# A decode-attention kernel: TensorE's closing part moved to the head of its program, one GpSimd library, x loaded by SyncE

## The chip, the core and the metric

The kernel runs on one core of one Trainium2 chip. The metric is the time of one execution on the device in microseconds (us), as the median of several runs. A core has five engines that run programs of their own and meet through semaphores: TensorE (PE in the profile, with PEld for its weight loads), VectorE (DVE), ScalarE (ACT), GpSimd (POOL) and SyncE (SP). Data moves between the main memory and the core's own memory through 16 DMA engines, which all queues share.

## What is computed

Two blocks of attention for one new token each, with the same shapes: a batch of 2, 32 heads, 8192 keys of 192 elements, a model width of 640, all bf16. `_B_ref` is the same as `_A_ref` here, since both have 32 heads of keys. The outputs of the two blocks are set side by side.

```python
q = (x @ wq).reshape(B, Sq, H, Dh).transpose(0, 2, 1, 3)          # x: 2 x 1 x 640, wq: 640 x 6144
scores = jnp.einsum("bhqd,bhkd->bhqk", q, k_cache) * (Dh ** -0.5) # k_cache: 2 x 32 x 8192 x 192
p = _softmax(scores, axis=-1)
o = jnp.einsum("bhqk,bhkd->bhqd", p, v_cache)
out = o.transpose(0, 2, 1, 3).reshape(B, Sq, H * Dh) @ wo         # wo: 6144 x 640
...
return jnp.concatenate([a, b], axis=-1)
```

## The kernel before

**Tiling.** The heads are taken in pairs: 2 blocks x 2 rows of the batch x 16 pairs are 64 pairs. For one pair, k (and likewise v) is one load of 6 MB: 128 partitions of 128 keys of 192 elements, the upper 64 partitions for one head, the lower 64 for the other. Three tiles `ring` take turns: the two large pieces of wq (4 of 5 rows per partition), then k and v of the pairs in order, at the end the pieces of wo. The fifth rows of wq go to the two tiles `prod`, which later hold products.

**Order of the work.** Each engine's instructions are collected in a `_Stream` in program order, with the keys that each waits for and the key that it signals; `reg` maps a key to a semaphore and a value. `emit` writes a stream out. For TensorE, VectorE and ScalarE it writes the part ahead of the loop (setup, projections and pair 0), a hardware loop `eng.Fori` of 21 passes over three pairs each (`LOOP`), and then the closing part, `self.run(eng, self.ops[at[n]:], {})`. SyncE and GpSimd have their streams written out without a loop.

**Start.** SyncE issues the loads in order (`load_on`, L196): A's large piece of wq, A's fifth rows, B's large piece, B's fifth rows, the first k; the next v waits until A's projection has read its slot, and so on. The load of the fifth rows waits for key `("x",)`. ScalarE issues the two small loads of x (L240) on its own queue. GpSimd fills the constants: the identity `ident` (a memset and an affine select, L402 and L403), `sel`, `place`, zeros for `pb` and so on, and signals `init` at its end (L418). TensorE opens the accumulation tile `oall` (L424, waits for `init`), transposes x (`fn_x`, L429; ScalarE copies it to `xT`) and projects each block in 12 groups of 5 matmuls (L260), which ScalarE copies to `qrow`.

**One pair.** VectorE multiplies k with the broadcast q in four quarters (L291); TensorE sums the 192 products in 12 matmuls of 16 columns a quarter (L296); VectorE reduces the rest (L302) and takes the maximum (L307, L308); GpSimd spreads the maximum over the partitions by `partition_all_reduce` (L311); ScalarE computes the exponentials (L323); TensorE multiplies with v in 64 matmuls (L335). TensorE also runs 12 matmuls on constants in each pair (`add_fill`, L343). The result of a pair is normalized on VectorE (L356 to L360) and put in its columns of `oall` by four small matmuls (`place`, L372) in the next pair.

**Closing part.** The last pair is placed (L372), `oall` is closed (L473) and copied to `oallS` (L378), and the 48 rows of wo of each block are contracted in 96 matmuls of 320 columns (L387), B's in eight pieces, so that the last ones can follow their loads; a few matmuls on constants stand between them. ScalarE copies each block's result out of `outps` (L395), and SyncE and ScalarE each issue one half of the output (L398).

Of the kernel before, what the change touches and what calls it, by code (L numbers as in the profile page):

```python
# [9 lines left out]
F32 = mybir.dt.float32  # L10


class _Stream:
# [40 lines left out]
            if has_sig:  # L54
                ins.then_inc(self.sem, 1)

    def emit(self, eng, loop=None):
        waited = {}
        if self.first:
            eng.sem_inc(self.sem, self.first)  # L60
        if loop is None:
            self.run(eng, self.ops, waited)
            return
        i0, step, n = loop
        at = [self.marks[i0 + step * t] for t in range(n + 1)]
        size = at[1] - at[0]
        passes = [self.ops[at[t]:at[t + 1]] for t in range(n)]
        needs = [[self.needs(w) for _, w, _ in ops] for ops in passes]
        delta = [{sid: needs[2][k][sid][1] - val for sid, (_, val) in need.items()} for k, need in enumerate(needs[1])]
        by, early = {}, {}  # L70
        for k, d in enumerate(delta):
            for sid, v in d.items():
                assert by.setdefault(sid, v) == v or not v or not by[sid]
                by[sid] = max(by[sid], v)
            for t, need in enumerate(needs):
                assert len(passes[t]) == size and passes[t][k][2] == passes[0][k][2]
                assert set(need[k]) == set(d) or t == 0 and set(need[k]) < set(d)
                for sid, (sem, val) in need[k].items():
                    plain = needs[1][k][sid][1] + (t - 1) * d[sid]
                    assert val == plain or t == 0 and val > plain  # L80
                    if val > plain:
                        early[sid] = (sem, max(val, early.get(sid, (sem, 0))[1]))
        self.run(eng, self.ops[:at[0]], waited)
        for sid, (sem, val) in early.items():
            if val > waited.get(sid, 0):
                eng.wait_ge(sem, val)
                waited[sid] = val
        for k, need in enumerate(needs[1]):
            for sid, (sem, val) in need.items():
                if not delta[k][sid] and val > waited.get(sid, 0):  # L90
                    eng.wait_ge(sem, val)
                    waited[sid] = val
        with eng.Fori(0, n) as t:
            base = {sid: eng.snap(t * d) for sid, d in by.items() if d}
            waited = {}
            for k, (fn, _, has_sig) in enumerate(passes[0]):
                for sid, (sem, val) in needs[1][k].items():
                    at0 = val - delta[k][sid]
                    if delta[k][sid] and at0 > waited.get(sid, 0):
                        eng.wait_ge(sem, base[sid] + at0)  # L100
                        waited[sid] = at0
                    assert not delta[k][sid] or at0 > 0
                ins = fn(eng, t)
                if has_sig:
                    ins.then_inc(self.sem, 1)
        self.run(eng, self.ops[at[n]:], {})


def build_kernel(nc, blocks, out):
    NBLK = len(blocks)  # L110
# [10 lines left out]
    LOOP = (1, STEP, 21)  # L121
# [5 lines left out]
    N = Hn * Dh  # L127
    RW = T * Dh
# [13 lines left out]
    with ExitStack() as es:  # L142
        sb = lambda name, shape, dt: es.enter_context(nc.sbuf_tensor(name, shape, dt))
# [8 lines left out]
        prod = [sb(f"prod{i}", [128, TQ * Dh], BF16) for i in range(2)]  # L152
# [9 lines left out]
        xr = sb("xr", [4, D], BF16)  # L162
# [5 lines left out]
        oallS = [sb(f"oallS{k}", [128, WR, 2], BF16) for k in range(NBLK)]  # L168
        out_sb = [sb(f"out_sb{k}", [34, NH2], BF16) for k in range(NBLK)]
        actd = sb("actd", [128, 2], F32)  # L170

        scps = [ps(f"scps{i}", [128, TQ, DG], F32) for i in range(2)]
        ops = [ps(f"ops{i}", [128, 512], F32) for i in range(NB)]
# [4 lines left out]
        reg = {}  # L178
        S_sp = _Stream("sp", sem("s_sp"), reg)
        S_pe = _Stream("pe", sem("s_pe"), reg, FIRST)  # L180
        S_act = _Stream("act", sem("s_act"), reg, FIRST)
        S_dve = _Stream("dve", sem("s_dve"), reg, FIRST)
        S_pool = _Stream("pool", sem("s_pool"), reg, FIRST)
        rsem = [sem(f"rsem{i}") for i in range(3)]
        psem = [sem(f"psem{i}") for i in range(2)]
        xsem = sem("xsem")
# [3 lines left out]
        def load(key, slot, out_ap, in_ap, waits):  # L190
            rcount[slot] += 16
            reg[key] = (rsem[slot], rcount[slot])
            load_on(out_ap, in_ap, rsem[slot], waits)

        def load_on(out_ap, in_ap, s, waits=()):
            S_sp.add(lambda eng, t: eng.dma_start(out_ap, in_ap).then_inc(s, 16), waits=waits)  # L196
# [8 lines left out]
        def next_slot(n=[0]):  # L205
            n[0] += 1
            return (n[0] - 1) % 3

        for blk in range(NBLK):
            w = blocks[blk]["wq"].rearrange("(j c) n -> j (c n)", c=DC)  # L210
            s = next_slot()
            load(("wq", blk), s, ring[s][:], w[:, 0:RW], [])
            reg[("wq5", blk)] = (psem[blk], 16)
            load_on(prod[blk][:, 0:N], w[:, RW:RW + N], psem[blk], [("x",)])
            free[s] = [("pr", blk, NQC - 1)]

        order = []
# [10 lines left out]
        for blk, pieces in ((0, WA), (1, WB)):  # L228
            w = blocks[blk]["wo"].rearrange("(p r) n -> p (r n)", r=WR)
# [4 lines left out]
                for r in range(r0, r1):  # L234
                    wo_at[blk, r] = ring[s][:, (at + r - r0) * D:(at + r - r0 + 1) * D]

        reg[("x",)] = (xsem, 32)
        for blk in range(NBLK):
            reg[("odone", blk)] = (osem[blk], 32)
            S_act.add((lambda blk: lambda eng, t: eng.dma_start(  # L240
                xr[2 * blk:2 * blk + 2, :], blocks[blk]["x"][:, 0, :]).then_inc(xsem, 16))(blk))

        def quarter(i, qd):
            return ring[slot_of["k", i]][:, qd * TQ * Dh:(qd + 1) * TQ * Dh].rearrange("p (t d) -> p t d", d=Dh)
# [138 lines left out]
        def add_contract(blk, r0, r1):  # L383
# [10 lines left out]
            if r1 == WR:  # L394
                S_act.add(lambda eng, t: eng.activation(out_sb[blk][:], outps[0:34, 0:NH2], ACTF.Identity),  # L395
                          waits=[("c", blk), ("init",)], sig=("oev", blk))
                for S, h in ((S_act, 0), (S_sp, 1)):
                    S.add((lambda h: lambda eng, t: eng.dma_start(  # L398
                        out[:, 0, blk * D + h * NH2:blk * D + (h + 1) * NH2],
                        out_sb[blk][32 * h:32 * h + 2, :]).then_inc(osem[blk], 16))(h), waits=[("oev", blk)])  # L400

        S_pool.add(lambda eng, t: eng.memset(ident[:], 1.0), sig=("id0",))  # L402
        S_pool.add(lambda eng, t: eng.affine_select(out=ident[:], in_=ident[:], compare_op=ALU.is_equal, fill=0.0, base=0,  # L403
                                                 pattern=[[-1, 128]], channel_multiplier=1), waits=[("id0",)], sig=("id",))
# [22 lines left out]
        def fn_x(eng, t):  # L427
            for c in range(DC):
# [4 lines left out]
                  waits=[("xp",)], sig=("xT",))  # L433
# [51 lines left out]
        with nc.Block() as block:  # L485
            @block.sync
            def _(eng):
                S_sp.emit(eng)

            @block.gpsimd  # L490
            def _(eng):
                S_pool.emit(eng)

            @block.vector
            def _(eng):
                S_dve.emit(eng, LOOP)

            @block.scalar
            def _(eng):
                S_act.emit(eng, LOOP)  # L500

            @block.tensor
            def _(eng):
                S_pe.emit(eng, LOOP)


def bass_concat_heads__gqa_block_cached__mha_block_cached__decode_kernel(
    nc: bass.Bass,
    A_x: bass.AP,
    A_k_cache: bass.AP,  # L510
    A_v_cache: bass.AP,
    A_wq: bass.AP,
    A_wo: bass.AP,
    B_x: bass.AP,
    B_k_cache: bass.AP,
    B_v_cache: bass.AP,
    B_wq: bass.AP,
    B_wo: bass.AP,
    out: bass.AP,
):  # L520
    blocks = [
        dict(x=A_x, k=A_k_cache, v=A_v_cache, wq=A_wq, wo=A_wo),
        dict(x=B_x, k=B_k_cache, v=B_v_cache, wq=B_wq, wo=B_wo),
    ]
    build_kernel(nc, blocks, out)
# [28 lines left out]
```

## Time and profile before

| what | value |
|---|---|
| median of 3 timed runs | 1939.19 us (1938.48 to 1939.3) |
| profiled execution, its own span from the first to the last instruction | 1937.5 us |
| TensorE matmul busy | 1634.4 us (84%) |
| VectorE busy | 1081.2 us (56%) |
| ScalarE busy | 188.2 us (10%) |
| GpSimd busy | 31.9 us (2%) |
| read from main memory | 836.77 MB, 432 GB/s over the span |
| first DMA issue, last DMA issue | 0.79 us, 1935.75 us |

The profile is of one execution, whose time is known by its span; the timed runs are others. Times in the profile are in us from the start of the span. A row of the timeline or of the grouped views gives the line of the kernel, the engine, the operation, the tile that is written and the tiles that are read, a count, and in brackets the idle time of the engine ahead of it with what ended that. A row of windows gives for each engine the busy time and in brackets the number of instructions, then TensorE's granted clock, the share of the 16 DMA engines that was busy, and GB/s. In the DMA table a queue's row gives packets, MB and the share of 16 engines' time; its "instruction" queues carry the engines' programs.

### The profile page before, as it was taken

How to read it: one execution, taken by the hardware profiler on the slowest of the kernel's cores; microseconds unless marked ns; L12 is line 12 of the kernel's file. 1: busy time of each engine (PE TensorE's matmuls, PEld its weight loads, DVE VectorE, ACT ScalarE, POOL GpSimd, SP SyncE). 2: the span in 40 equal slices, each digit the busy share in tenths (PEclk: the TensorE clock that was granted, in tenths of full speed). 3: DMA queues.
4: the chain of work that ended last, by engine and by line, in shares of the span. 5: the costliest groups of instructions: out<-in, count | busy, mean ns of one | idle time of the engine just before them, and what ended most of it. 6: DMA issues, size and time to landing. Idle time of an engine off the chain costs nothing.

```text
span 1937.5 us, 21660 instructions
## 1 busy us (share of the span) xinstructions
PE 1634.4 (84%) x8652; PEld 788.0 (41%) x8717; DVE 1081.2 (56%) x834; ACT 188.2 (10%) x612; POOL 31.9 (2%) x88
## 2 busy tenths in 40 slices
PE   4888888888888888888888888888888888888888
PEld 1344443443443443443443443443443443443444
DVE  0556546546556646646656646646656645645652
ACT  2111011011011011011011011011011001001000
POOL 1000000000000000000000000000000000000000
PEclk9999999999999999999999999999999999999999
DMA  9999999999999999999999999999999999999998
GB/s 415 429 433 435 435 429 435 437 432 432 435 437 428 435 436 434 429 436 437 430 432 436 434 429 436 436 434 430 436 436 429 434 436 434 429 436 436 433 431 382
DMA packets 20627, 836.93 MB, mean 432 GB/s; under 512 B 2300, under 2 KB 2568, under 8 KB 2952
## 3 DMA queue, kind: packets, MB, share of 16 engines
q1 hardware_dynamic: 20600, 836.78, 99.8%
q8 instruction: 7, 0.11, 0.0%
q14 instruction: 4, 0.03, 0.0%
q10 hardware_dynamic: 16, 0.01, 0.0%
HBM read 836.77 MB, written 0.01 MB: 432 GB/s over the span
## 4 chain that ended last, share of the span: by engine, by line
issue 92%; PE 3%; DMA 3%; POOL 1%; DVE 1%; ACT 0%; POOLq 0%; SPq 0%; ACTq 0%; DVEq 0%
DMA ring<-in_B_wq_dram 1%; POOL mg L311 1%; PE ops L335 1%; DMA ring<-in_B_wo_dram 1%; PE ops L260 1%; DVE prod L291 1%; PE scps L296 1%; DMA xr<-in_B_x_dram 0%; DVE sc L302 0%; ACT pb L323 0%; PE outps L387 0%; SPq L196 0%; POOLq L49 0%; PE scps L343 0%; ACT qrow L266 0%
## 5 line engine op out<-in xcount | busy, mean ns | idle before, releaser
L291 DVE TENSOR_TENSOR prod<-ring,qt 128x6144 bf16<-128x6144 bf16 x256 | 852.6, 3351 | 694.9 <-DMA ring<-in_B_k_cache_dram 331.1
L296 PE MATMUL scps<-prod,ident 128*128 128x512 bf16 x3072 | 709.2, 381 | 199.2 <-DVE prod L291 199.2
L335 PE MATMUL ops<-ring,pb 128*34 128x384 bf16 x4096 | 676.8, 326 | 0.0
L296 PEld LDWEIGHTS scps<-prod,ident 128*128 128x128 bf16 x3072 | 280.4, 98 | 604.7 <-DVE prod L291 298.8
L335 PEld LDWEIGHTS ops<-ring,pb 128*34 128x34 bf16 x4096 | 395.5, 98 | 258.7
L302 DVE TENSOR_REDUCE sc<-scps 128x32 f32<-128x512 f32 x256 | 175.3, 685 | 112.0 <-PE scps L296 112.0
L343 PE MATMUL outps<-filler,ident 128*128 128x512 bf16 x704 | 162.4, 379 | 10.1 <-issue 10.0
L343 PEld LDWEIGHTS outps<-filler,ident 128*128 128x128 bf16 x768 | 70.0, 98 | 78.2
L352 ACT ACTIVATE oodd<-ops 2x192 f32<-2x192 f32 x64 | 20.6, 322 | 690.4 <-PE ops L335 690.4
L284 ACT ACTIVATE qt<-qps 64x192 bf16<-64x192 f32 x66 | 21.4, 324 | 676.3 <-PE qps L278 676.3
L323 ACT ACTIVATE pb<-sc,nb 64x128 bf16<-64x128 f32 x128 | 81.4, 636 | 8.0
L348 PE MATMUL ops<-ones,rs 128*2 128x1 f32 x128 | 12.2, 164 | 61.5 <-ACT pb L323 61.5
L311 POOL PARTITION_ALL_REDUCE mg<-mp x64 | 22.8, 356 | 1860.2 <-DVE mp L308 1860.2
L348 PEld LDWEIGHTS ops<-ones,rs 128*2 128x2 f32 x128 | 5.5, 82 | 93.1 <-ACT pb L323 93.1
L316 ACT ACTIVATE nb<-mg 64x1 f32<-64x1 f32 x64 | 13.0, 203 | 310.7 <-POOL mg L311 310.7
L323 ACT ACTIVATION_READ_ACCUMULATOR pb<-sc,nb 64x1 f32 x128 | 38.4, 300 | 0.0
L260 PE MATMUL ops<-ring,xT 128*2 128x512 bf16 x96 | 28.6, 426 | 6.0 <-issue 4.2
L307 DVE TENSOR_REDUCE mp<-sc 64x1 f32<-64x128 f32 x64 | 17.8, 278 | 10.7 <-DVE sc L302 5.4
L278 PE MATMUL qps<-qrow,sel 34*128 (+1 forms) x66 | 22.0, 333 | 1.4 <-ACT qt L285 0.8
L372 PEld LDWEIGHTS oall<-on,place 2*128 (+1 forms) x256 | 10.3, 92 | 28.2 <-issue 26.7
L285 ACT ACTIVATE qt<-qps 64x192 bf16<-64x192 f32 x66 | 21.5, 326 | 0.8
L358 DVE TENSOR_TENSOR oodd<-ops,oodd 2x192 f32<-2x192 f32 x64 | 20.9, 326 | 0.2 <-ACT oodd L352 0.2
(43 smaller groups left out, 161.2 us busy)
## 6 DMA issues: line engine op xcount, KB each, us to landing
ring<-in_A_k_cache_dram SPq DMA_DIRECT2D x32, 6144.0 KB, 26.2
ring<-in_A_v_cache_dram SPq DMA_DIRECT2D x32, 6144.0 KB, 29.1
ring<-in_B_k_cache_dram SPq DMA_DIRECT2D x32, 6144.0 KB, 26.2
ring<-in_B_v_cache_dram SPq DMA_DIRECT2D x32, 6144.0 KB, 29.1
ring<-in_A_wq_dram SPq DMA_DIRECT2D x1, 6144.0 KB, 17.6
ring<-in_B_wq_dram SPq DMA_DIRECT2D x1, 6144.0 KB, 28.5
ring<-in_A_wo_dram SPq DMA_DIRECT2D x2, 3040.0 KB, 22.3
ring<-in_B_wo_dram SPq DMA_DIRECT2D x1, 2240.0 KB, 23.2
```

Source lines behind the costliest of these rows:

```text
L260: ins = eng.matmul(ops[n % 2][32 * blk:32 * blk + 2, 0:QC], xT[:, c, 2 * blk:2 * blk + 2], src, start=(c == 0), stop=(c == DC - 1))
L278: return eng.matmul(qps[:, 0:2 * Dh], sel[:].rearrange("p s m -> p (s m)")[:, bass.ds(k, 128)], qrow[:, bass.ds(c, 2 * Dh)], start=True, s ...
L284: eng.activation(qt[i % 3][0:64, :], qps[0:64, 0:Dh], ACTF.Identity)
L285: return eng.activation(qt[i % 3][64:128, :], qps[64:128, Dh:2 * Dh], ACTF.Identity)
L291: S_dve.add(lambda eng, t: eng.tensor_tensor(pr3(qd), quarter(i, qd), q, ALU.mult), waits=w, sig=("m", i, qd))
L296: ins = eng.matmul(scps[qd % 2][:], ident[:], pr3(qd)[:, :, j * DG:(j + 1) * DG], start=(j == 0), stop=(j == NJ - 1))
L302: S_dve.add(lambda eng, t: eng.tensor_reduce(sc[i % NB][:, qd * TQ:(qd + 1) * TQ], scps[qd % 2][:], AXL.X, ALU.add), waits=[("s", i, qd), ...
L311: S_pool.add(lambda eng, t: eng.partition_all_reduce(mg[i % NB][:], mp[i % NB][:], 128, bass.bass_isa.ReduceOp.max), waits=[("mx", i), key ...
L323: ins = eng.activation(pb[i % NB][p0:p0 + 64, :, h::32], sc[i % NB][p0:p0 + 64, :].rearrange("p (j a) -> p j a", a=2), ACTF.Exp, bias=nb[i ...
L335: ins = eng.matmul(ops[i % NB][0:34, 0:2 * Dh], pb[i % NB][:, j, :], vv[:, j, :], start=(j == 0), stop=(j == T // 2 - 1))
L343: ins = eng.matmul(to, ident[:], filler[:], start=True, stop=True)
L358: S_dve.add(lambda eng, t: eng.tensor_tensor(oodd[i % NB][:], ops[i % NB][0:2, 0:Dh], oodd[i % NB][:], ALU.add), waits=[("od", i)], sig=(" ...
```

## The change

Four edits. (1) `emit` takes an optional `nc`; with it, TensorE's program begins with a jump to a part `main`; behind the jump stands the part `close` with the closing instructions and a jump to `end`; then `main`, which holds what stood ahead of the closing part (now in a method `rolled`) and ends with a jump to `close`; `end` follows. Only TensorE's stream is given `nc`. (2) GpSimd's first two operations are a memset of a small new tile `warm` and a `partition_all_reduce` on it, ahead of the first affine select. (3) SyncE issues the two loads of x, right behind A's large piece of wq, in place of ScalarE. (4) The loads of the fifth rows of wq no longer wait for x.

```diff
-    def emit(self, eng, loop=None):
+    def emit(self, eng, loop=None, nc=None):
...
+        if nc is not None:
+            names = [f"{self.name}_{x}" for x in ("main", "close", "end")]
+            eng.br(names[0])
+            with nc.body(names[1], valid_engines=[eng.engine]):
+                self.run(eng, self.ops[at[n]:], {})
+                eng.br(names[2])
+            with nc.body(names[0], valid_engines=[eng.engine]):
+                self.rolled(eng, at, n, passes, needs, delta, by, early, waited)
+                eng.br(names[1])
+            nc.switch_bb(names[2])
+            return
+        self.rolled(eng, at, n, passes, needs, delta, by, early, waited)
+        self.run(eng, self.ops[at[n]:], {})
+
+    def rolled(self, eng, at, n, passes, needs, delta, by, early, waited):
         self.run(eng, self.ops[:at[0]], waited)
...
-        self.run(eng, self.ops[at[n]:], {})
...
+        warm = sb("warm", [128, 2], F32)
...
+        reg[("x",)] = (xsem, 32)
         for blk in range(NBLK):
...
             load(("wq", blk), s, ring[s][:], w[:, 0:RW], [])
+            if not blk:
+                for k in range(NBLK):
+                    load_on(xr[2 * k:2 * k + 2, :], blocks[k]["x"][:, 0, :], xsem)
             reg[("wq5", blk)] = (psem[blk], 16)
-            load_on(prod[blk][:, 0:N], w[:, RW:RW + N], psem[blk], [("x",)])
+            load_on(prod[blk][:, 0:N], w[:, RW:RW + N], psem[blk])
...
-        reg[("x",)] = (xsem, 32)
         for blk in range(NBLK):
             reg[("odone", blk)] = (osem[blk], 32)
-            S_act.add((lambda blk: lambda eng, t: eng.dma_start(
-                xr[2 * blk:2 * blk + 2, :], blocks[blk]["x"][:, 0, :]).then_inc(xsem, 16))(blk))
...
+        S_pool.add(lambda eng, t: eng.memset(warm[:], 0.0), sig=("warm",))
+        S_pool.add(lambda eng, t: eng.partition_all_reduce(warm[:, 1:2], warm[:, 0:1], 128, bass.bass_isa.ReduceOp.max),
+                   waits=[("warm",)])
...
-                S_pe.emit(eng, LOOP)
+                S_pe.emit(eng, LOOP, nc)
```

## The prediction

> **What bounds the kernel now.** I read the page's slices first, then the grouped DMA table of three stretches, then the queue's waits, then the first 60 us and the last 60 us of the timeline.
>
> ```profile
> span 1937.5 us, 21660 instructions
> ...
> DMA  9999999999999999999999999999999999999998
> GB/s 415 429 433 435 435 429 435 437 432 432 435 437 428 435 436 434 429 436 437 430 432 436 434 429 436 436 434 430 436 436 429 434 436 434 429 436 436 433 431 382
> ...
> HBM read 836.77 MB, written 0.01 MB: 432 GB/s over the span
> ```
>
> The transfers are never idle. The middle slices lie at 428 to 437 GB/s, and only the first (415) and the last (382) fall short. The DMA table of the stretch from 190 to 1915 us gives the steady rate:
>
> ```profile
> DMA packets 17393, 748.10 MB, mean 434 GB/s; under 512 B 1933, under 2 KB 1933, under 8 KB 1933
> ...
> q1 hardware_dynamic: 17391, 748.08, 100.2%
> q14 instruction: 2, 0.02, 0.0%
> ```
>
> 836.77 MB at 434 GB/s are 1928.0 us of the 1937.5 us span. So 9.5 us are left for everything else: the start, the end, and the uneven finish of the 16 engines. The page's landing times say how deep the queue is:
>
> ```profile
> ring<-in_B_k_cache_dram SPq DMA_DIRECT2D x32, 6144.0 KB, 26.2
> ring<-in_B_v_cache_dram SPq DMA_DIRECT2D x32, 6144.0 KB, 29.1
> ```
>
> One such load is 6.29 MB, 14.5 us at 434 GB/s. A load of k that lands 26.2 us after its issue has 11.7 us of other transfers ahead of it when it is issued, so TensorE, which frees its slot, could be some 11 us later in any pair without a gap. The body of the program is therefore out of the change's reach; only start and end count. The end, from the timeline:
>
> ```profile
> 1883.74 6.62 DVE L291 TENSOR_TENSOR prod<-ring,qt 128x6144 bf16<-128x6144 bf16 x2 [10.29 <-DMA ring<-in_B_k_cache_dram]
> ...
> 1916.53 0.27 PE L372 MATMUL oall<-on,place 2*128 2x48 bf16 x4 [1.14 <-DVE on L360]
> ...
> 1917.35 6.68 PE L387 MATMUL outps<-ring,oallS 128*2 128x320 bf16 x96 [0.46 <-ACT oallS L378]
> ...
> 1930.94 0.98 PE L387 MATMUL outps<-ring,oallS 128*2 128x320 bf16 x12 [0.18 <-DMA ring<-in_B_wo_dram]
> ...
> 1932.88 0.84 PE L387 MATMUL outps<-ring,oallS 128*2 128x320 bf16 x10 [0.21 <-DMA ring<-in_B_wo_dram]
> ...
> 1934.41 0.84 PE L387 MATMUL outps<-ring,oallS 128*2 128x320 bf16 x10
> ...
> 1935.75 0.25 ACTq L398 DMA_DIRECT2D out_dram<-out_sb  x1
> ```
>
> The last load of k lets VectorE start at 1883.74; from there a serial chain of 53.8 us leads to the end. In the closing part TensorE waits for pieces of wo only 0.18 + 0.21 = 0.39 us, so chain and transfers end within half a microsecond of each other, and both hang on the landing of the slowest DMA engine. How uneven the engines are, in four windows of 1 us:
>
> ```profile
> 1931.00:1932.00 1.00, 1.00 (x13) 0.49 (x14) 0.00 (x0) 0.00 (x0) 0.00 (x0) 1.00 0.98 385
> 1932.00:1933.00 1.00, 0.79 (x5) 0.19 (x5) 0.00 (x0) 0.00 (x0) 0.00 (x0) 1.00 0.67 255
> 1933.00:1934.00 1.00, 1.00 (x12) 0.47 (x9) 0.00 (x0) 0.00 (x0) 0.00 (x0) 1.00 0.25 92
> 1934.00:1935.00 1.00, 1.00 (x13) 0.34 (x10) 0.00 (x0) 0.00 (x0) 0.00 (x0) 1.00 0.03 12
> ```
>
> The share (last column but one) falls to 0.67, 0.25 and 0.03 (half an engine): some engines are done before 1932.5 and one works until about 1934.5 (0.03 of 16 engines for 1 us is one engine for half a microsecond). 0.98 + 0.67 + 0.25 + 0.03 = 1.93, so 16 even engines would be done at 1932.9. **1.6 us is the most that evening them out can bring.**
>
> **Part 1: TensorE's closing part stands first.** It adds two jumps at the head (to the body, and over the closing part), one to the closing part behind the loop, one to the end. It removes nothing. Three things are to be costed.
>
> The jump to the closing part, and the fetching of instructions:
>
> ```profile
> q8 instruction: 5, 0.08, 0.2%
> ...
> q8 instruction: 2, 0.03, 0.5%
> ...
> L93 PEldq COMPARE_BRANCH x21: 76/208/238, 173.7 to 1912.4; - x21
> ```
>
> The first row is the DMA table from 50 to 190 us, the second that from 1915 to 1938 us; from 190 to 1915 us no q8 packet stands in its table above. So blocks of 0.11 MB / 7 = 16 KB are fetched while TensorE goes through new code, none while it repeats the loop, and two more in the closing part. A backward branch, whose target is held, takes 208 ns; the last one, not taken, 76 ns. It stands at 1912.4, and the first closing matmul waits for VectorE until 1916.53. TensorE's sequencer is thus **4.1 us ahead**, and this covers the new jump: 0.2 us where the block is still held, and a fetch where it is not. The two packets took 0.5% of 16 engines x 23 us = 1.84 us, 0.92 us each; with the wait behind one bulk packet (6.29 MB in 128 rows is 49 KB on an engine of 27 GB/s, 1.8 us, an estimate) 2.7 us. Value: 0; if the 4.1 us did not cover, the fetch less 4.1 us and less the 0.39 us of slack above.
>
> [...]
>
> The two packets of the tail move to the start, where the jump over the closing part makes TensorE draw them early. On the slowest engine they would give back 1.84 us, capped at the 1.6 us above; on another nothing, or they make another engine the slowest: 0 to 0.9 us lost. Average over 16 engines: 1.84 / 16 = **0.1 us gained**, the value I take. The jump at the head costs nothing: TensorE's first work waits for `init` until 19.87 (below).
>
> **Part 2: one GpSimd library.** The rows of its two loads, the stall, and the operation that is added:
>
> ```profile
> L403 POOLq MODIFY_POOL_CONFIG  x2: 12/12/12, 1.1 to 1.1; - x2
> L311 POOLq MODIFY_POOL_CONFIG  x2: 1/1/1, 20.0 to 20.0; - x2
> L311 POOL PARTITION_ALL_REDUCE mg<-mp x64: 355/356/376, 79.7 to 1902.4; - x64
> 10.99 0.28 POOL L403 TENSOR_SCALAR_AFFINE_SELECT ident<-ident 128x128 bf16<-128x128 bf16 x1 [9.92 <-issue]
> 19.87 0.34 PE L424 MATMUL oall<-place 2*128 2x192 bf16 x1 [19.87 <-POOL mp L418]
> 22.09 1.86 PE L260 MATMUL ops<-ring,xT 128*2 128x512 bf16 x4 [1.73 <-DMA prod<-in_A_wq_dram]
> 41.47 1.86 PE L260 MATMUL ops<-ring,xT 128*2 128x512 bf16 x4 [4.22 <-issue]
> ```
>
> The load at 1.1 (9.92 us) stays, for the all-reduce instead of the select; the one at 20.0 goes. It was hidden: the first all-reduce comes at 79.7. On POOL a small memset (0.1, an estimate) and one all-reduce (0.36) are put ahead, so `init` comes about 0.5 us later, at 20.4. Behind it in TensorE's program stand L424, the transpose of x and the projections, which start at 22.09 because the last part of A's wq lands; TensorE idled 1.73 us before that. 0.5 us is covered. Were that cover gone, the 4.22 us of idle time before B's projection come next. Value on POOL: 0.
>
> [...]
>
> What the second load cost the transfers no view shows directly. Bound: the windows of 14 us before and after.
>
> ```profile
> 22.00:36.00 14.00, 13.91 (x55) 5.03 (x56) 0.00 (x0) 5.87 (x10) 0.00 (x0) 1.00 0.95 406
> 36.00:50.00 14.00, 9.78 (x34) 3.22 (x33) 0.00 (x0) 3.88 (x7) 0.00 (x0) 0.76 1.04 447
> ```
>
> The share is 0.95 behind the load and 1.04 later; packets are booked whole, so most of this is counting. At most 0.05 x 14 = 0.7 us is gained, at least 0; a loss has no row for it, as the load only goes. I take 0.3.
>
> **Part 3: x on SyncE's queue.**
>
> ```profile
> 0.79 0.40 SPq L196 DMA_DIRECT2D ring<-in_A_wq_dram  x1
> 1.45 7.40 DMA xr<-in_B_x_dram
> 8.86 0.35 SPq L196 DMA_DIRECT2D prod<-in_A_wq_dram  x1
> ...
> ring<-in_A_wq_dram SPq DMA_DIRECT2D x1, 6144.0 KB, 17.6
> ...
> prod<-in_A_wq_dram SPq DMA_DIRECT2D x1, 1536.0 KB, 13.1
> ```
>
> Removed: SyncE's wait for x (until 8.86). Its four next issues (the rest of A's wq, both of B's, the first k) come some 6 us earlier, two issues of x by 0.35 us behind the first. Nothing lands earlier by that: A's first piece lands at 0.79 + 17.6 = 18.4, and the next, 1.57 MB (3.6 us at 434 GB/s), at 8.86 + 13.1 = 22.0. It follows without a gap already. Price: x now lies behind the first piece in the same queue and lands at about 18.4 instead of 8.85. TensorE needs it after `init` (20.4): covered by 2 us. Even 7.40 us for it, as on ScalarE's queue, counted from 18.4, means 25.8, 3.7 us late for the projections, less than the 4.22 us idle before B. ScalarE's queue keeps the outputs alone. Value: 0.
>
> **Sum.** 1937.5 - 0.1 - 0.3 + 0 = 1937.1 us of span. The median of the three timed runs, 1939.19, is 1.69 above that profiled span; I carry this along: **1938.8 us**. About 0.2% (3.9 us) is what a measurement of this kernel can tell from no change, ten times this.
>
> **The rivals.**
> - The slowest engine is relieved in full (the second library load or the tail's fetches lay on it): the whole 1.6 us, 1937.6. For it: one engine alone works after 1934. Against: 15 others could be the ones hit.
> - The moved fetches hit a slow engine: all seven packets now come before the last k, one of 0.92 us more on it and no relief: 1939.19 + 0.92 = 1940.1. Nothing in the views says which engine takes one.
> - Slower: the loop no longer fits. Moved behind the closing part, it may reach over five blocks where it reached over four. If the store of instructions holds fewer than that, each of 21 passes fetches five blocks: 105 x 16 KB = 1.72 MB, 4.0 us at 434 GB/s, 1943.2 if spread evenly, some 10 us if bunched on a few engines (1949). It decides from one block too few. Against: no fetch at all in twenty passes. In the same family, a jump at 1912.4 that has to fetch and takes as long as x's 7.40 us: 7.40 - 4.1 - 0.4 = 2.9, 1942.1.
> - It doesn't do what it says: the select belongs to another library, which is loaded again. Then `init` comes 10.3 us later (9.92 + 0.36), at 30.2, and the projections some 9 us later; 4.2 us of that go into the idle time before B, and 4.7 us delay the first pairs, against a queue some 11 us deep in steady state whose depth at the start these rows do not give: 0 to 4.7 us, 1940.5 for a quarter of it.
>
> **How the numbers follow.** Chances: forecast 0.66, relieved 0.12, moved fetches 0.09, fetch at the jump or in the loop 0.08 (half of it over 0.2%), library twice 0.05. Within half a microsecond of the forecast, timed runs scatter anyway (1938.48 to 1939.3). The range takes in the relieved case and the moved fetches and half of the library case: 1937.2 to 1940.6. Faster by over 0.2% would need more than the 1.6 us that the uneven engines hold: 0.03, out of the relieved case, for a relief that these views do not show. Slower by over 0.2%: 0.06, half of the case of the fetches (0.04) and the costly end of the library case (0.02). Within: 0.91.
>
> **What would show it.** Right: SP's wait for x gone, x landing near 18.4, one pair of MODIFY_POOL_CONFIG, `init` near 20.4, A's projection at 22 as before; q8 packets all before 190 us and none in the closing part; the first closing matmul 1.1 us behind the last PV one. Wrong: q8 packets between 190 and 1915 us, an idle stretch of "issue" on TensorE ahead of L372, the first projection later than 26 us, or a load of k landing with a gap in the transfers before 110 us.

## The result, and the profile after

| kernel | median | lowest to highest | runs |
|---|---|---|---|
| before | 1938.86 us | 1938.48 to 1939.33 | 21 |
| after | 1941.99 us | 1941.37 to 1943.3 | 21 |

The change makes the kernel slower by 3.1 us: the ratio is 1.0017, with a 95% interval of 1.0011 to 1.0023. The forecast of 1938.8 us and its range of 1937.2 to 1940.6 are both missed. The profiled execution of the changed kernel took 1941.58 us; its page gives a span 2.4 us longer than before, and a last slice at 360 GB/s instead of 382. The profiled execution of before (span 1937.5 us, as runs of 1939.2 to 1939.3 us have it) is one of that kernel's longer ones and this one is among the shorter ones of its kernel, so the two profiles differ by less than the medians do.

```profile
span 1939.9 us, 21728 instructions
...
GB/s 418 429 432 434 436 432 433 435 436 433 432 435 435 434 432 435 436 434 432 434 436 434 432 434 436 434 433 433 436 434 433 433 437 434 432 434 436 435 432 360
```

The slices between stand at 429 to 437 GB/s, much as before, so the time went at the end. There the new branch is the first thing to look at. This is the view of one line's instructions: line, queue, operation, count, least / median / longest time in ns, and when the first and the last of them stood.

```profile
L91 PEldq COMPARE_BRANCH  x1: 5869/5869/5869, 1911.8 to 1911.8; - x1
L108 PEldq COMPARE_BRANCH  x21: 76/208/248, 171.9 to 1911.7; - x21
```

L91 is the jump from the end of the loop to the closing part, L108 the loop's own branch. The jump took 5.87 us, until 1917.7, where a branch within the loop takes 0.21. The DMA tables of three stretches of the changed kernel (0 to 30, 50 to 190 and 1910 to 1945 us) say why; from 190 to 1910 us its table has no q8 row:

```profile
q8 instruction: 2, 0.03, 0.4%
...
q8 instruction: 5, 0.08, 0.2%
...
q8 instruction: 3, 0.05, 0.5%
```

Seven blocks of TensorE's program are fetched before the jump, two of them at the start, where the kernel before has no such row. Yet three more are fetched from the jump on, so what stood at the head of the program was no longer held. Cut into windows of 0.2 us, the table shows a single q8 packet within the jump, in the window of 1915.2 to 1915.4:

```profile
q8 instruction: 1, 0.02, 29.1%
```

29.1% of 16 engines x 0.2 us are 0.93 us, which the table books whole in one window. So the block itself is a small part of the 5.87 us: 3.4 us of the jump lie ahead of that window and 2.3 us behind it. What fills them, no view shows. The end of the timeline, to be set beside the one of before:

```profile
1883.01 3.36 DVE L307 TENSOR_TENSOR prod<-ring,qt 128x6144 bf16<-128x6144 bf16 x1 [10.31 <-DMA ring<-in_B_k_cache_dram]
...
1915.44 0.31 DVE L376 TENSOR_SCALAR on<-oodd,rc 2x192 bf16<-2x192 f32 x1
...
1917.86 0.25 PE L388 MATMUL oall<-on,place 2*128 2x48 bf16 x4 [3.20 <-issue]
...
1918.66 8.22 PE L403 MATMUL outps<-ring,oallS 128*2 128x320 bf16 x96 [0.46 <-ACT oallS L394]
...
1936.73 0.84 PE L403 MATMUL outps<-ring,oallS 128*2 128x320 bf16 x10
...
1938.08 0.25 ACTq L414 DMA_DIRECT2D out_dram<-out_sb  x1
```

VectorE has the last pair ready at 1915.75 (1915.44 + 0.31), but TensorE starts to place it only at 1917.86: 3.20 us idle, and the bracket names no other engine or transfer, only "issue". Before, it idled 1.14 us there and VectorE ended that. The contraction of A behind it takes 8.22 us for the same 96 matmuls that took 6.68. The last group waits for nothing, where before pieces of wo held up the groups ahead of it. The chain that ended last, first of before, then of after, shows the exchange:

```profile
1916.27 16.56 DMA ring<-in_B_wo_dram
```

```profile
1915.75 2.11 issue
1917.86 0.25 PE oall L388 x4
...
1918.67 8.23 PE outps L403 x96
...
1936.80 0.79 PE outps L403 x10
```

Before, the last pieces of wo set the end. Now TensorE's own chain does, from a wait of 2.11 us for its instructions on. The transfers are almost done by the time that the last groups run:

```profile
1934.00:1935.00 1.00, 1.00 (x11) 0.33 (x7) 0.00 (x0) 0.00 (x0) 0.00 (x0) 1.00 0.11 42
```

The longer contraction is a matter of the clock: between the two stretches below it stands at 0.50 throughout. Windows of 0.2 us of the changed kernel (the granted clock is the third number from the end):

```profile
1918.20:1918.40 0.20, 0.00 (x1) 0.00 (x0) 0.00 (x0) 0.16 (x2) 0.00 (x0) 1.00 0.83 358
1918.40:1918.60 0.20, 0.00 (x0) 0.00 (x0) 0.00 (x0) 0.20 (x2) 0.00 (x0) 0.53 0.99 422
...
1921.60:1921.80 0.20, 0.20 (x4) 0.08 (x2) 0.00 (x0) 0.00 (x0) 0.00 (x0) 0.50 1.05 448
1921.80:1922.00 0.20, 0.20 (x6) 0.14 (x4) 0.00 (x0) 0.00 (x0) 0.00 (x0) 0.94 0.90 384
```

The clock falls to half at 1918.41 and comes back at 1921.82 (a window at 0.53 held the full clock for 0.06 of it, one at 0.94 half the clock for 0.12 of it). That is 3.41 us at half speed, of which 3.16 lie in the contraction and cost half of that, 1.58; 8.22 - 6.68 = 1.54 was measured.

So the two profiled executions differ like this: the last k comes 0.73 us earlier in this execution (1883.74 - 1883.01), the wait for instructions and the rest up to the placement add 2.06 (placement 1.33 later, although k was 0.73 earlier), the half clock 1.54, and 0.52 is absorbed because TensorE no longer waits for wo. -0.73 + 2.06 + 1.54 - 0.52 = 2.35 against 1938.08 - 1935.75 = 2.33 at the last DMA issue. Without the -0.73, which the runs below do not tie to any part of the change, the terms give 3.08.

The start changed too:

```profile
L419 POOLq MODIFY_POOL_CONFIG  x2: 11/11/11, 1.0 to 1.0; - x2
```

```profile
1.69 0.29 POOL L422 TENSOR_SCALAR_AFFINE_SELECT ident<-ident 128x128 bf16<-128x128 bf16 x1
...
10.56 0.34 PE L443 MATMUL oall<-place 2*128 2x192 bf16 x1 [10.56 <-POOL mp L437]
...
18.14 0.35 PE L448 MATMUL qps<-ident,xr 4*128 4x4 bf16 x5 [7.24 <-DMA xr<-in_B_x_dram]
...
23.11 1.86 PE L276 MATMUL ops<-ring,xT 128*2 128x512 bf16 x4 [4.62 <-DMA prod<-in_A_wq_dram]
```

One pair of library operations is left, the stall of 9.92 us ahead of the select is gone, `init` comes at 10.56 instead of 19.87, x lands at 18.14, and the projection starts 1.0 us later than before.

### The profile page after: what moved, and what is told of

Same layout as the page of the kernel before. It is cut to its first block, busy times and chain, and to the rows that moved or that the text cites. A ratio compares the mean times of both kernels' runs of the same rounds, so it can differ in the third digit from the quotient of the medians.

```text
span 1939.9 us, 21728 instructions
## 1 busy us (share of the span) xinstructions
PE 1644.6 (85%) x8717; PEld 788.0 (41%) x8717; DVE 1081.2 (56%) x834; ACT 188.0 (10%) x612; POOL 32.2 (2%) x90
## 4 chain that ended last, share of the span: by engine, by line
issue 92%; PE 4%; POOL 1%; DMA 1%; DVE 1%; ACT 0%; POOLq 0%; SPq 0%; DVEq 0%; ACTq 0%
PE ops L276 2%; POOL mg L327 1%; DMA prod<-in_A_wq_dram 1%; PE ops L351 1%; PE outps L403 1%; DVE prod L307 1%; PE scps L312 1%; DVE sc L318 0%; PE scps L359 0%; ACT pb L339 0%; POOLq L49 0%; SPq L211 0%; ACT out_sb L411 0%; ACT qrow L282 0%; DVE mp L324 0%
## 5 line engine op out<-in xcount | busy, mean ns | idle before, releaser
L359 PE MATMUL outps<-filler,ident 128*128 128x512 bf16 x768 | 176.9, 380 | 0.0
```

What stands on the lines that cost most here:

```text
L359: ins = eng.matmul(to, ident[:], filler[:], start=True, stop=True)
```

## The experiments

The theory was: TensorE's memory for instructions does not hold the whole program; the block with the closing part, drawn first, is displaced by the last block of the loop, so the jump has to fetch under a full stream of transfers (435 GB/s from 1911.8 to 1917.7 in the changed kernel), for longer than the 4 us of cover, and the idle time halves the clock. The rivals: a far jump is slow by itself; the time comes from the other parts of the change; the slow contraction has another cause than the idle time. The kernels ran in two groups, beside runs of before with medians of 1938.85 and 1938.87 us.

**The change without part 1.** The closing part goes back behind the loop.

```diff
-                S_pe.emit(eng, LOOP, nc)
+                S_pe.emit(eng, LOOP)
```

> The changed kernel with TensorE's closing part behind the loop again; the library and the loads of x stay as changed. Theory (the jump to the closing part is fetched, 5.9 us, and TensorE's idle time halves its clock): no idle stretch of issue ahead of L388, the contraction of A back at 6.7 us, and the 0.7 us by which the last k landed earlier in the changed kernel stay: about 1938.2 us, 0.7 under the kernel before. Rival (the loss comes from the moved loads or the library): as slow as the changed kernel, 1942.

Measured: 1938.49 us (1938.05 to 1938.62), ratio to before 0.9998 (0.9989 to 1.0007). Its timeline:

```profile
1915.71 0.27 PE L388 MATMUL oall<-on,place 2*128 2x48 bf16 x4 [1.14 <-DVE on L376]
...
1916.52 6.68 PE L403 MATMUL outps<-ring,oallS 128*2 128x320 bf16 x96 [0.46 <-ACT oallS L394]
```

The idle time is 1.14 us again, ended by VectorE, and the contraction takes 6.68. Part 1 thus accounts for the whole loss of 3.1 us and a little more (1941.99 - 1938.49 = 3.5 us).

**Part 1 alone.** The kernel before with the new order of TensorE's program and nothing else.

```diff
-                S_pe.emit(eng, LOOP)
+                S_pe.emit(eng, LOOP, nc)
```

> The kernel before with TensorE's closing part first, nothing else. Theory (fetch): two GpSimd library loads as before, so the last k lands near 1883.7 as before; a jump of 5 to 7 us at 1912.4, 2 us of idle time and 1.5 us of slower contraction, less 0.4 to 0.5 us of slack: 1938.9 + 3.1 = 1942.0 or more (to 1943). Rival (moved loads): 1938.9, no change.

Measured: 1942.49 us (1941.76 to 1943.32), ratio 1.0018 (1.0009 to 1.0027). Its branch, its contraction, and the windows in which the clock falls and rises:

```profile
L91 PEldq COMPARE_BRANCH  x1: 5809/5809/5809, 1911.9 to 1911.9; - x1
```

```profile
1918.83 9.18 PE L401 MATMUL outps<-ring,oallS 128*2 128x320 bf16 x96 [0.46 <-ACT oallS L392]
```

```profile
1917.00:1917.20 0.20, 0.00 (x0) 0.00 (x0) 0.00 (x0) 0.00 (x0) 0.00 (x0) 0.83 0.83 358
...
1923.80:1924.00 0.20, 0.20 (x4) 0.13 (x2) 0.00 (x0) 0.00 (x0) 0.00 (x0) 0.60 0.91 384
```

Part 1 alone brings the whole loss. The jump costs as much (5.81 us), but the clock stays halved from 1917.13 to 1923.96, 6.83 us, twice as long as in the changed kernel, and the contraction loses 2.50 us instead of 1.54. One point of the expectation was missed: the last k was to land as before, near 1883.7, as there are two library loads. It landed 0.6 us earlier:

```profile
1883.10 3.36 DVE L305 TENSOR_TENSOR prod<-ring,qt 128x6144 bf16<-128x6144 bf16 x1 [10.27 <-DMA ring<-in_B_k_cache_dram]
```

So the 0.73 us by which it came earlier in the changed kernel cannot be put down to the library. Two executions of the same instructions up to there, of the kernel before and of the one with the late VectorE below, have it at 1883.74 and 1883.30, and the shorter program below, with one library load, at 1883.71.

**The closing part between pair 0 and the loop.** A far jump stays: back over the whole loop. But the closing part is drawn later than the program's head. `head` holds what stood ahead of the loop, `rolled` the loop alone.

```diff
+            self.head(eng, at, needs, delta, early, waited)
             eng.br(names[0])
             with nc.body(names[1], valid_engines=[eng.engine]):
...
-                self.rolled(eng, at, n, passes, needs, delta, by, early, waited)
+                self.rolled(eng, n, passes, needs, delta, by)
                 eng.br(names[1])
```

> The changed kernel with the closing part placed between pair 0 and the loop instead of at the head (the jump over it stands ahead of the loop). Theory (the store of instructions has lost the first block by the end of the loop, but still holds the blocks right ahead of the loop): the jump to the closing part takes 0.2 us, no q8 packet falls into the closing part, about 1938.2 us. Rival (any jump back out of the loop is fetched, near or far): jump of 5 to 7 us, three q8 packets behind it, 1942.

Measured: 1938.47 us (1938.16 to 1938.64), ratio 0.9998 (0.9989 to 1.0007). The branch, and the q8 rows of 30 to 50 and 50 to 190 us; later there is none, in the closing part neither:

```profile
L92 PEldq COMPARE_BRANCH  x1: 169/169/169, 1911.8 to 1911.8; - x1
```

```profile
q8 instruction: 1, 0.02, 0.3%
...
q8 instruction: 6, 0.10, 0.3%
```

A jump back over the whole loop takes 0.17 us where its target is held. This run also prices the two fetches of the tail that the prediction hoped to be rid of. They are gone here and not in the kernel without part 1, and the medians are 1938.47 and 1938.49: no difference that these runs could tell from scatter.

**The closing part first, in a shorter program.** The change, with fewer matmuls on constants in TensorE's program (they add nothing to the result): none in pair 0, 6 instead of 12 in the later pairs, none in the closing part. 84 instructions go, not the 78 that the expectation names.

```diff
-            add_fill(i)
+            if i:
+                add_fill(i, 6)
...
-            if k in (2, 3, 4, 5):
-                add_fill(NP + k, 3, scps[0].rearrange("p t g -> p (t g)"), [("r", LAST, 3)])
```

> The changed kernel, closing part still first, with 78 instructions fewer on TensorE, all of them matmuls on constants: none in pair 0 and in the closing part, 6 instead of 12 in each other pair (they add nothing to the result). By the times of the q8 packets the loop then ends some ten to forty instructions short of the place at which the seventh packet was drawn. Theory (the last packet drawn in the loop's first pass overwrites the first block): six q8 packets before 190 us instead of seven, the jump takes 0.2 us, no fetch behind it, contraction at full clock: about 1938, if the clock holds with fewer matmuls on constants. Rival (any jump back out of the loop is fetched): jump of 5 to 7 us, 1941 to 1942.

Measured: 1938.48 us (1938.04 to 1941.01), ratio 1.0000 (0.9991 to 1.0009). The branch, the q8 row of 50 to 190 us (with 2 from 0 to 30 and none after 190) and the contraction:

```profile
L91 PEldq COMPARE_BRANCH  x1: 169/169/169, 1912.6 to 1912.6; - x1
```

```profile
q8 instruction: 4, 0.07, 0.2%
```

```profile
1917.39 6.68 PE L403 MATMUL outps<-ring,oallS 128*2 128x320 bf16 x96 [0.46 <-ACT oallS L394]
```

The same order with the same jump, in a program that draws six packets ahead of the jump instead of seven: the closing part is still held. That is the test of the displaced block. With fewer matmuls on constants the mean granted clock of the profiled execution is 0.972 instead of 0.997, but the contraction runs at full clock. Two of its ten runs (1940.35 and 1941.01) lie above the others; no trace of them is on record, so what made them longer stays open.

**The jump after the cover.** The change, with the first two closing operations (the placement and the closing matmul of `oall`) kept behind the loop, ahead of the jump.

```diff
-                self.run(eng, self.ops[at[n]:], {})
+                self.run(eng, self.ops[at[n] + 2:], {})
...
+                self.run(eng, self.ops[at[n]:at[n] + 2], {})
                 eng.br(names[1])
```

> The changed kernel with the last placement and the closing matmul of oall left behind the loop, so that the jump to the rest of the closing part comes behind them. Theory (fetch of fixed length from the moment of the jump; the sequencer is held by the wait for VectorE until 1915.8): placement at 1.1 us behind the last PV matmul as in the kernel before, jump at about 1916, the contraction of A starts about 1922 instead of 1918.7: about 3.3 us more than the changed kernel, 1945. Rival (the closing part's first wait, not the fetch, holds TensorE): no change, 1942.

Measured in four runs: 1945.41 us (1944.4 to 1945.92), ratio 1.0032 (1.0018 to 1.0047).

```profile
L92 PEldq COMPARE_BRANCH  x1: 6089/6089/6089, 1916.0 to 1916.0; - x1
```

```profile
1922.28 8.93 PE L404 MATMUL outps<-ring,oallS 128*2 128x320 bf16 x96 [5.98 <-issue]
```

```profile
1920.00:1920.20 0.20, 0.00 (x0) 0.00 (x0) 0.00 (x0) 0.00 (x0) 0.00 (x0) 0.67 1.26 538
...
1926.80:1927.00 0.20, 0.20 (x6) 0.13 (x4) 0.00 (x0) 0.00 (x0) 0.00 (x0) 0.76 0.79 333
```

The fetch takes as long as at the other place (6.09 us) and now stands almost whole on the path: TensorE idles 5.98 us of "issue", of which it would have spent 0.46 us on waiting for ScalarE's copy anyway. In the change TensorE idled 2.06 us longer than before, so just under 4 us of the fetch were covered there, as the prediction's cover said. The clock is halved from 1920.07 to 1926.90, again 6.83 us.

**The idle time without a fetch.** The kernel before, with VectorE made late by one memset of a tile that is not used any more; TensorE's program is untouched.

```diff
+        S_dve.add(lambda eng, t: eng.memset(qrow[:], 0.0), waits=[("pv", LAST)])
```

> The kernel before with a memset of 2.6 us (qrow, no longer read) put on VectorE ahead of the last pair's normalization: TensorE is idle 3.7 us ahead of the placement, without any jump. Theory (an idle time of some 3 us halves TensorE's clock): windows with a granted clock of 0.50 for about 3 us, the contraction of A 8.2 us instead of 6.7, in all 2.6 + 1.5 - 0.4 = 3.7 us more: 1942.6. Rival (the slow contraction in the changed kernel was its fetches): contraction 6.7 us, clock 1.00, 2.2 us more: 1941.1.

Measured: 1943.75 us (1942.66 to 1944.22), ratio 1.0024 (1.0014 to 1.0034).

```profile
1919.07 0.34 PE L372 MATMUL oall<-on,place 2*128 2x48 bf16 x4 [4.11 <-DVE on L360]
...
1920.03 9.50 PE L387 MATMUL outps<-ring,oallS 128*2 128x320 bf16 x96 [0.46 <-ACT oallS L378]
```

```profile
1918.80:1919.00 0.20, 0.00 (x0) 0.00 (x0) 0.20 (x1) 0.00 (x0) 0.00 (x0) 0.97 1.35 576
...
1925.80:1926.00 0.20, 0.20 (x6) 0.11 (x4) 0.00 (x0) 0.00 (x0) 0.00 (x0) 0.96 0.93 397
```

Here TensorE waits for VectorE and not for instructions, and its clock halves all the same, so the fetch is not needed for that. Half speed lasts from 1918.99 to 1925.82, 6.83 us, so the contraction takes 9.50 us, more than was expected.

**One library alone, and x on SyncE alone.** The kernel before with part 2 only (the `warm` tile and its two operations), and with parts 3 and 4 of the edits only.

```diff
+        S_pool.add(lambda eng, t: eng.memset(warm[:], 0.0), sig=("warm",))
+        S_pool.add(lambda eng, t: eng.partition_all_reduce(warm[:, 1:2], warm[:, 0:1], 128, bass.bass_isa.ReduceOp.max),
+                   waits=[("warm",)])
```

> The kernel before with the all-reduce on a small tile ahead of GpSimd's first select, nothing else. Theory (the second library load disturbed some DMA engines, among them the slowest): init near 10.6 instead of 19.9, the last k lands about 0.7 us earlier, 1938.2 us. Rival (the 0.7 us come from x): 1938.9.

```diff
+            if not blk:
+                for k in range(NBLK):
+                    load_on(xr[2 * k:2 * k + 2, :], blocks[k]["x"][:, 0, :], xsem)
...
-            load_on(prod[blk][:, 0:N], w[:, RW:RW + N], psem[blk], [("x",)])
+            load_on(prod[blk][:, 0:N], w[:, RW:RW + N], psem[blk])
```

> The kernel before with x loaded by SyncE behind the first piece of wq and no wait for x, nothing else. Theory (the gain is the library's): two library loads as before, 1938.9 us, within 0.3. Rival (the gain is x's, whose packets on another queue held up two or three DMA engines): about 1938.2.

Measured: 1938.51 us (1938.28 to 1938.74) with one library, ratio 0.9998 (0.9989 to 1.0007); 1938.97 us (1938.65 to 1939.44) with x on SyncE, ratio 1.0000 (0.9991 to 1.0009). The first select in the one and in the other:

```profile
1.69 0.29 POOL L421 TENSOR_SCALAR_AFFINE_SELECT ident<-ident 128x128 bf16<-128x128 bf16 x1
```

```profile
11.98 0.28 POOL L418 TENSOR_SCALAR_AFFINE_SELECT ident<-ident 128x128 bf16<-128x128 bf16 x1 [10.91 <-issue]
```

The stall at entry goes when the second library goes, not with x. The four kernels that have one library and no missing block (the one with one library alone, the one without part 1, the one with the closing part in the middle, the one with the shorter program) have medians of 1938.47 to 1938.51, some 0.36 us under before. They are the quickest measured here, but each interval contains 1, so a gain is likely and not shown. The last k lands at 1883.13 with one library and at 1883.65 with x on SyncE, as the theory had it, but the executions named under part 1 alone do not sort by the library in this way.

## Why the prediction was wrong, and where it was right

**What failed: part 1, "4.1 us ahead ... covers".** The cover was sized rightly: the jump stood at 1911.8, VectorE was done at 1915.75, 3.9 us. The fetch was not. The prediction's 2.7 us were 0.92 for a block and 1.8 for one bulk packet ahead of it; a jump that has to fetch takes 5.81 to 6.09 us in three kernels. The 0.92 was right (0.93 in the changed kernel), so the term that was mis-sized is the rest, the waiting: 4.9 us instead of 1.8. It put the jump at 0 where TensorE idled 2.06 us longer. The sum also has no term for the clock, which halved after that idle time and cost 1.54 us more. The sign that the prediction itself named for being wrong, a stretch of "issue" on TensorE ahead of the placement, is what the trace shows. The price was built from packets of fetches for which, in the profile of before, no engine was seen to stand and wait. A small transfer that an engine did wait for in that profile, x with 7.40 us, was the better measure. For the jump, the prediction used it in a rival only.

**The rival that came true** was the jump at 1912.4 that has to fetch: 7.40 - 4.1 - 0.4 = 2.9, 1942.1 us. The time fits (1941.99), its terms do not: the fetch was 1.5 shorter, and the halved clock, which it left out, cost 1.54 in the profiled execution. The two misses cancelled, so its time was right by luck. That a far jump is slow by itself is not what the runs show: with the closing part in the middle or in the shorter program, the jump over the whole loop took 0.17 us. With the closing part at the head, seven packets drawn ahead of the jump made it a fetch of 5.81 to 6.09 us, and six did not (0.17 us). How much of its program TensorE can hold, no run shows.

**The loop.** That it is held was right: no q8 packet from 190 to 1910 us. The rival of a loop that no longer fits, 1943.2 to 1949 us, is refuted; that one block too few would make each pass fetch all five was its assumption, which no run shows.

**The tail's fetches moved to the start.** "q8 packets all before 190 us" was wrong, three came in the closing part. Where they did go, no gain shows, 0.02 us against the 0.1 of the sum, but runs of one kernel scatter more than either. At the start there is something that the prediction did not have: "A's projection at 22 as before" was wrong. It stands at 22.64 to 23.11 in the four kernels whose closing part is at the head, which draw two packets before 30 us, against 21.87 to 22.09 in the others, which draw none. That the packets delay the loads is the author's reading of this order; no run shows it by itself. The end of the program does not show the delay: the last k lands at 1883.01 in the change and at 1883.74 before.

**Part 2.** The gain of 0.3 us for the library was right in size as far as the runs can tell (0.36, interval above). "The load at 1.1 (9.92 us) stays" and `init` at 20.4 were wrong: the stall vanished and `init` came at 10.56. TensorE gained nothing by that, as it waited for x and wq anyway. The stall went with the second library, as the two selects above show (1.69 and 11.98); why, no run shows. The rival that the select loads a second library is refuted by the single pair of MODIFY_POOL_CONFIG. (Its 1940.5 us for a quarter of 4.7 us should have been 1940.4: 1939.19 + 1.2.)

**Part 3.** Right: x at 18.14 (about 18.4 was predicted), value 0 (1938.97 against 1938.87).

**The slack of 0.39 us** that TensorE had behind wo was taken off the rival's loss rightly: 0.52 was absorbed.

## What to carry to other kernels

A jump back to code that may no longer be held has to be priced as a transfer that someone waits for, and not by the length of its packet: here it took 5.81 to 6.09 us in three kernels, where 2.7 were predicted. Idle time of TensorE of 3.14 to 5.98 us ahead of the closing part's matmuls cost its length here and then half of the time from the start of the contraction to the return of the clock, measured as 1.54 to 2.82 us; a sum that adds such a gap needs a term for it. Here the loop was the last to draw new blocks ahead of the jump: code placed just ahead of it was held (a jump of 0.17 us) and code placed first was not (5.87 us), and one packet fewer, six instead of seven, decided it (0.17 us).

## What the runs showed of the hardware

The half clock lasted 3.41 us in the changed kernel and 6.83 us in three others, once and twice the same length, and its end did not follow the first matmul at a fixed distance: 3.16 us after the contraction's start in the change, 5.13 with part 1 alone, 4.62 with the late jump, 5.79 with the late VectorE. Half of each, 1.58, 2.57, 2.31 and 2.90 us, is the loss, and 1.54, 2.50, 2.25 and 2.82 were measured over the 6.68. Why it lasted this long, and once or twice it, no run shows. The idle time ahead of the placement was 3.20 us in the changed kernel and the clock fell; it was 1.14 us before and the clock stayed at 1.00. With part 1 alone the clock fell at 1917.13, only 2.38 us after TensorE went idle at 1914.75 (1917.89 - 3.14).

The runs of the changed kernel spread over 1.9 us, and those of before over 0.85: eleven runs of the changed kernel lie at 1941.37 to 1941.99, the profiled one with its 3.41 us of half clock among them, and ten at 1942.33 to 1943.3. Whether the clock stayed halved for longer in those ten is not known, as their traces are not there to show it.
